# Decoding 64-bit weights with two VectorE instructions, and parts made on GpSimd and ScalarE

## The chip, the cores and the metric

The kernel runs on one core of a Trainium2 chip. The metric is the device time of one launch in microseconds (us). TensorE (PE in the profile) does the matrix products, VectorE (DVE), ScalarE (ACT) and GpSimd (POOL) work on elements, and SyncE (SP) issues most of the transfers (DMAs).

## The reference

The first half is a gated linear recurrence with a complex state, over 4 sequences, 8 heads, 768 steps and width 48; its output, laid out as 3072 tokens of 384, goes through a feed-forward layer.

```
mag = np.sqrt(a_re * a_re + a_im * a_im)
scale = np.minimum(mag, 0.999) / (mag + 1e-06)
a_re_n, a_im_n = (a_re * scale, a_im * scale)
for t in range(S):
    S_re, S_im = (ar * S_re - ai * S_im) + kv, ar * S_im + ai * S_re
    y[:, :, t] = np.einsum('bhd,bhde->bhe', q[:, :, t], S_re)
...
h = np.maximum(x @ w_in, 0.0)
return (h * h @ w_out).astype(np.float32)
```

The weights w_in (384 x 2048) and w_out (2048 x 384) arrive as 64-bit floats, which the kernel sees as pairs of 32-bit words, low and high. It must turn them into 32-bit floats on the chip.

## The kernel before

The tokens are worked in 12 groups, each of two chunks of 128 tokens. A group goes through these steps. Operands (23 small steps, `make_operands`): the gates are squared, limited and scaled on ScalarE and VectorE (`limit` and `lessened`, through the helper at L684, make two factors on ScalarE that `gates`, L750, reads, and `grown_factor`, L744, a third; `grown_squared`, L763, squares the key growth; `grow`, L770, is a scan of it); `totals`, `carries`, `carried` and `products` then form running products of the gates in a long row of short VectorE instructions (helper line L480, most of them with the names ab and pr), and end with the group's keys and queries, qk. Chunks: TensorE turns the keys (L878, tp), ScalarE copies them (L882 and L883, kt), TensorE makes scores (L871, a_ps), VectorE multiplies them by the mask (a<-a_ps,mask), TensorE makes the outputs (L863 and L897, y) and adds to the state (L918, add). GpSimd makes some small products of the last rows (L923 and L924, prod<-last), which wait for a transfer last<-qk. Then the feed-forward layer: the first product (L960, h_ps, eight pieces F0 to F7 of a group, which hold the buffers of h_ps two at a time), squared ReLU on ScalarE (L963 to L966, H), the second product. Groups 0 and 1 do the second product piece by piece with each w_out block (L976, o_ps, token T); later groups do it in seven smaller products over sums of halves (L1042). Outputs are copied from PSUM by ScalarE or added by VectorE (L996 to L998 and L1046 to L1066).

The weights come in 16 blocks of 128 x 768 pairs of words, eight of w_in (`order` "1") and then eight of w_out ("2"). `fetch` (L610) brings a block into one of three buffers called words; for w_in half of it goes through GpSimd's queue (token j, L632), the rest and all of w_out through SP's (token f, L626 and L632). `decode` (L579 to L595) turns a block into floats by five VectorE instructions: L586 and L588 build the head of the float from the high word (shift by 3, mask, sign), L590 keeps its power of two, L593 scales the low word with it, and the helper at L480 adds both into the weights w. `watch` (token W, L597 to L601) makes two ScalarE passes over each block, whose sums tell later whether the values lie in the range that this path handles; if they don't, a general path at the end of the program does everything anew. With these inputs it isn't entered.

The order of the work on all five engines is written out by hand. A string, FRONT (L1076), lists tokens, a letter and numbers each, and `follow` (L1196) issues them in turn: o0.8 is operand step 8 of group 0, a1.5 and b1.5 are chunk steps, l and i load a group's raw input (SP's and GpSimd's queue), D5 decodes block 5, W5 watches it, F0.6 is a piece of the first product, T0.0 one of the second. Each engine runs its instructions in the order in which they are issued. F0.k needs weights of D0 to Dk; T with index f needs D of 8 plus f. In the first stretch the tokens around the decodes run as follows; the full string has no decode beyond D15, which ends ahead of group 3.

```
D0 o0.9 o0.10 o0.6 o0.11 W0 W1 D1 o0.22 f3 v1 j3 o0.12 W2 o0.13 o0.15 o0.14 f4 j4 W3
l1 i1 o0.16 W4 o0.17 D2 o0.18 o1.6 o0.19 f5 j5 o0.20 o1.0 W5 a0.1 o1.3 o0.21 o1.1 D3
```

Of the kernel before, what the change touches and what calls it, by code (L numbers as in the profile page):

```python
# [23 lines left out]
I32 = mybir.dt.int32  # L24
U32 = mybir.dt.uint32
# [4 lines left out]
P = 128  # L30
# [395 lines left out]
def quotient_path(ctx, tc, feat, vtok, w_in, w_out, w1, w2, out, n_seq, count):  # L426
# [151 lines left out]
    order = "1111111122222222"  # L578
    def decode(dst, words, j):  # L579

        low, high = words[:, :, 0], words[:, :, 1]
        both = scr.tile([P, 2, E], I32, tag="work", name="decoded")
        head, rest = both[:, 0], both[:, 1]
        nc.vector.tensor_scalar(out=head, in0=high, scalar1=3, scalar2=0x3FFFFFF8,  # L586
                                op0=ALU.logical_shift_left, op1=ALU.bitwise_and)
        nc.vector.scalar_tensor_tensor(out=head, in0=high, scalar=-2 ** 30, in1=head,  # L588
                                       op0=ALU.bitwise_and, op1=ALU.bitwise_or)
        nc.vector.tensor_scalar(out=rest, in0=head, scalar1=-2 ** 23, scalar2=None,  # L590
                                op0=ALU.bitwise_and)
        rest = rest.bitcast(F32)
        nc.vector.scalar_tensor_tensor(out=rest, in0=low.bitcast(U32), scalar=2.0 ** -52, in1=rest,  # L593
                                       op0=ALU.mult, op1=ALU.mult)
        tt(dst, head.bitcast(F32), rest, ALU.add)  # L595
# [40 lines left out]
    def weights(i):  # L636
        if i in words_of:
            of_w2, j = block(i)
            decode(w2[:, 2 * j:2 * j + 2].rearrange("p k m -> p (k m)") if of_w2 else
                   w1[:, :, j * BLK:(j + 1) * BLK], words_of[i], i)  # L640
# [304 lines left out]

    h_ps, h_of, o_of, mix_of = {}, {}, {}, {}
# [16 lines left out]
    def squared_relu(i, f):  # L963
        h = h_of[i, f] = ffn.tile([P, 2, TOK], F32, name="h", bufs=NFB // 2 + 1)
        nc.scalar.activation(out=h, in_=h_ps[i, f], func=AF.Relu)  # L965
        nc.scalar.activation(out=h, in_=h, func=AF.Square)  # L966
# [29 lines left out]
    def end_of_second(i, b):  # L996
        out_of[i, b] = ffn.tile([P, DM], F32, name="o")
        nc.scalar.copy(out=out_of[i, b], in_=o_of[i, b])  # L998
# [47 lines left out]
    def outputs(i, r):  # L1046
# [6 lines left out]
        if r == 0:  # L1053
            nc.scalar.copy(out=o[0][:, left], in_=chain)
        elif r == 1:
            tt(o[0][:, left], others[0], o[0][:, left], ALU.add)
        elif r == 2:
            nc.scalar.copy(out=o[0][:, right], in_=chain)
        elif r == 3:
            nc.scalar.copy(out=o[1][:, right], in_=others[1])  # L1060
        elif r == 4:
            tt(o[1][:, right], chain, o[1][:, right], ALU.add)
        elif r == 5:
            tt(o[0][:, right], others[1], o[0][:, right], ALU.add)
        else:
            nc.scalar.copy(out=o[1][:, left], in_=chain)  # L1066
# [11 lines left out]
        "D0 o0.9 o0.10 o0.6 o0.11 W0 W1 D1 o0.22 f3 v1 j3 o0.12 W2 o0.13 o0.15 o0.14 f4 j4 W3 "  # L1078
        "l1 i1 o0.16 W4 o0.17 D2 o0.18 o1.6 o0.19 f5 j5 o0.20 o1.0 W5 a0.1 o1.3 o0.21 o1.1 D3 "
        "a0.2 a0.3 o1.4 o1.5 a0.4 a0.8 o1.2 o1.7 f6 j6 b0.0 a0.9 o1.8 b0.1 b0.2 b0.5 o1.9 b0.6 "  # L1080
        "D4 b0.3 b0.7 a0.0 b0.4 o1.10 W6 b0.8 o1.11 f7 j7 a0.5 o1.12 o1.22 a0.6 b0.9 o1.13 W7 "
        "a0.7 o1.15 o1.14 g0 v2 l2 i2 o1.16 F0.0 o1.17 F0.1 H0.0 D5 o1.18 F0.2 H0.1 o2.6 o1.19 "
        "f8 F0.3 H0.2 F0.4 H0.3 o1.20 o2.0 F0.5 H0.4 W8 a1.1 o2.3 o1.21 D6 a1.2 a1.3 o2.1 a1.4 "
        "a1.8 o2.4 o2.2 F0.6 D7 f9 H0.5 o2.5 a1.0 H0.6 a1.9 F0.7 a1.5 W9 f10 o2.7 a1.6 b1.1 "
        "a1.7 D8 b1.0 o2.10 o2.8 H0.7 b1.5 o2.9 f11 b1.6 D9 b1.2 b1.3 b1.7 T0.0 b1.4 g1 W10 "
        "o2.11 T0.1 W11 f12 F1.0 D10 o2.12 o2.22 F1.1 H1.0 D11 T0.2 H1.1 f13 W12 F1.2 o2.15 "
        "T0.3 H1.2 o2.13 F1.3 W13 f14 o2.16 o2.14 b1.8 F1.4 v3 H1.3 l3 b1.9 F1.5 H1.4 D12 W14 "
        "F1.6 D13 T0.4 f15 T1.0 H1.5 D14 F1.7 H1.6 T1.1 o3.6 o2.17 T1.2 H1.7 D15 W15 T1.3 o2.18 "
        "o2.19 T0.5 T0.6 t0 o3.0 T0.7 t1 T1.4 E0.0 t2 E0.1 s0.0 s0.1 o3.3 T1.5 o2.20 o3.4 o3.5 "
        "T1.6 o3.7 o3.1 o2.21 T1.7 o3.2 o3.10 a2.1 t3 E1.0 E1.1 s1.0 a2.2 s1.1 a2.0 o3.8 o3.9 "  # L1090
        "a2.3 a2.5 a2.4 a2.6 o3.11 a2.8 a2.7 b2.0 a2.9 o3.12 o3.22 b2.1 b2.5 b2.2 b2.6 o3.13 "
        "b2.3 b2.7 b2.4 g2 b2.8 o3.15 o3.14 v4 l4 F2.0 b2.9 F2.4 H2.0 o3.16 F2.1 H2.4 o3.17 "
        "F2.5 H2.1 X2.0 o3.18 Y2.0 o3.19 F2.2 H2.5 F2.6 H2.2 o4.6 o3.20 F2.3 H2.6 o4.0 F2.7 "
        "X2.1 o3.21 H2.3 Y2.1 o4.3 o4.1 X2.2 a3.1 Z2.0 o4.2 Y2.2 H2.7 a3.0 X2.3 o4.4 R2.0 Y2.3 "
        "a3.2 o4.5 a3.3 a3.5 Z2.1 a3.4 o4.7 a3.8 Q2.2 o4.10 Q2.1 R2.1 o4.8 a3.6 a3.9 Z2.2 a3.7 "
        "o4.9 Q2.3 Q2.0 b3.0 o4.11 R2.2 b3.1 Z2.3 b3.2 b3.5 o4.12 o4.22 o4.15 b3.6 R2.3 Z2.4 "
        "b3.7 g3 o4.13 Z2.5 R2.4 o4.14 o4.16 Z2.6 l5 b3.3 R2.6 R2.5 F3.0 b3.4 o4.17 b3.8 H3.0 "
        "F3.4 b3.9 o4.18 s2.0 o4.19 F3.1 H3.4 v5 s2.1 F3.5 H3.1 X3.0 o4.20 F3.2 H3.5 o5.6 F3.6 "
        "H3.2 X3.1 o4.21 o5.1 Y3.1 Y3.0 a4.1 F3.3 H3.6 X3.2 o5.2 Y3.2 F3.7 H3.3 a4.2 o5.0 a4.0 "
        "o5.3 H3.7 X3.3 o5.4 a4.3 Z3.0 a4.4 a4.5 o5.5 Y3.3 o5.7 a4.8 R3.0 a4.6 a4.9 o5.10 Z3.1 "  # L1100
        "a4.7 o5.8 o5.9 Z3.2 R3.1 Q3.2 Q3.1 Q3.0 Q3.3 o5.11 b4.0 R3.2 b4.1 b4.5 o5.12 Z3.3 "
        "o5.22 o5.15 b4.2 b4.6 R3.3 b4.3 b4.7 Z3.4 b4.4 g4 o5.13 b4.8 R3.4 o5.14 Z3.5 v6 b4.9 "
        "l6 o5.16 F4.0 Z3.6 H4.0 R3.5 o5.17 F4.4 R3.6 o5.18 s3.0 o5.19 s3.1 F4.1 H4.4 F4.5 H4.1 "
        "X4.0 o5.20 F4.2 H4.5 o6.6 F4.6 H4.2 X4.1 o5.21 Y4.1 o6.1 Y4.0 F4.3 H4.6 X4.2 o6.2 F4.7 "
        "Y4.2 H4.3 o6.0 a5.0 o6.3 H4.7 X4.3 o6.4 Z4.0 o6.5 a5.5 Y4.3 o6.7 a5.6 R4.0 Z4.1 a5.7 "
        "o6.10 o6.8 Z4.2 R4.1 Q4.2 o6.9 Q4.1 Q4.0 Q4.3 o6.11 b5.0 R4.2 Z4.3 b5.5 o6.12 o6.22 "
        "o6.15 b5.6 R4.3 Z4.4 b5.7 v7 g5 o6.13 Z4.5 R4.4 o6.14 o6.16 Z4.6 l7 F5.0 R4.5 R4.6 "
        "o6.17 F5.4 H5.0 o6.18 o6.19 F5.1 H5.4 s4.0 s4.1 F5.5 H5.1 X5.0 o6.20 F5.2 H5.5 o7.6 "
        "F5.6 X5.1 o6.21 H5.2 Y5.1 Y5.0 o7.1 a6.1 F5.3 H5.6 X5.2 o7.2 F5.7 Y5.2 H5.3 a6.2 a6.0 "
        "H5.7 X5.3 o7.0 a6.3 Z5.0 a6.5 a6.4 Y5.3 o7.3 a6.8 R5.0 o7.4 a6.6 a6.9 o7.5 Z5.1 a6.7 "  # L1110
        "o7.7 o7.10 Z5.2 R5.1 Q5.2 o7.8 Q5.1 Q5.0 Q5.3 o7.9 b6.0 o7.11 R5.2 b6.1 Z5.3 b6.2 b6.5 "
        "o7.12 b6.3 Z5.4 b6.4 o7.15 R5.3 o7.22 b6.6 b6.8 b6.7 g6 R5.4 Z5.5 o7.13 v8 Z5.6 b6.9 "
        "o7.14 R5.5 o7.16 s5.0 F6.0 R5.6 l8 o7.17 F6.4 H6.0 F6.1 H6.4 X6.0 o7.18 Y6.0 s5.1 F6.5 "
        "o7.19 H6.1 F6.2 H6.5 X6.1 F6.6 H6.2 Y6.1 o7.20 o8.6 F6.3 H6.6 o8.0 X6.2 o7.21 Y6.2 "
        "a7.1 o8.3 H6.3 F6.7 o8.1 Z6.0 H6.7 X6.3 o8.2 Y6.3 a7.0 R6.0 o8.4 a7.2 o8.5 a7.3 a7.5 "
        "Z6.1 a7.4 o8.7 Z6.2 R6.1 o8.10 Q6.2 Q6.1 o8.8 Q6.0 Q6.3 o8.9 a7.8 a7.6 a7.9 R6.2 Z6.3 "
        "a7.7 o8.11 b7.0 R6.3 o8.12 b7.1 b7.5 o8.22 Z6.4 o8.15 b7.2 b7.6 b7.3 b7.7 Z6.5 b7.4 g7 "
        "R6.4 o8.13 b7.8 R6.5 o8.14 Z6.6 v9 b7.9 s6.0 l9 o8.16 F7.0 R6.6 F7.4 H7.0 o8.17 F7.1 "
        "H7.4 X7.0 o8.18 s6.1 Y7.0 F7.5 o8.19 H7.1 F7.2 H7.5 X7.1 F7.6 H7.2 Y7.1 o8.20 o9.6 "
        "F7.3 H7.6 o9.0 X7.2 o8.21 Y7.2 a8.1 o9.3 H7.3 F7.7 o9.1 Z7.0 H7.7 X7.3 o9.2 Y7.3 a8.0 "  # L1120
        "R7.0 o9.4 a8.2 o9.5 a8.3 a8.5 Z7.1 a8.4 o9.7 Z7.2 R7.1 o9.10 Q7.2 Q7.1 o9.8 Q7.0 Q7.3 "
        "o9.9 a8.8 a8.6 a8.9 R7.2 Z7.3 a8.7 o9.11 b8.0 R7.3 o9.12 b8.1 b8.5 o9.22 Z7.4 o9.15 "
        "b8.2 b8.6 b8.3 b8.7 Z7.5 b8.4 g8 R7.4 o9.13 b8.8 R7.5 o9.14 Z7.6 v10 b8.9 s7.0 l10 "
        "o9.16 F8.0 R7.6 F8.4 H8.0 o9.17 F8.1 H8.4 X8.0 o9.18 s7.1 Y8.0 F8.5 o9.19 H8.1 F8.2 "
# [23 lines left out]
    def ranges(step):  # L1148
# [34 lines left out]
        "s": store,  # L1183
        "f": fetch,
        "j": lambda i: fetch(i, True),
        "i": lambda gi, part=None: load_parts(gi, part, True),
        "D": weights,
        "W": lambda i: watch(words_of[i], i) if i in words_of else None,
        "t": sum_weights,
# [70 lines left out]
```

## Time and profile before

| | us |
|---|---|
| median of 3 runs (701.58 to 702.04) | 701.61 |
| span of the profiled execution | 700.1 |
| what lies around the span, median less span | 1.5 |
| one decode on VectorE, start to the next start | 4.05 |
| VectorE busy in the first 200 us, by stages of 20 | 15.15, 19.03, 18.54, 18.75, 19.27, 18.06, 19.31, 19.10, 19.62, 14.43 |
| TensorE busy in the same stages | 0.47, 0, 6.82, 15.01, 16.10, 17.62, 20.00, 20.00, 20.00, 15.77 |
| TensorE busy from 200 to 650 | 448.90 |

The profile is of one execution, and its times count from the start of its span. A line such as `38.05 0.56 DVE L586 TENSOR_SCALAR decoded<-words 128x768 int32` is one instruction or a row of equal ones: start, duration, engine, line of the kernel, operation, output and inputs, shape and type, count; a bracket at its end gives the idle time of the engine ahead of it and what ended it. Records of the helper at L480 are told apart by their tiles.

### The profile page before, as it was taken

To read this page: it belongs to the slowest core of one execution; us is meant where nothing else is said; L and a number is where in the kernel's file an instruction comes from. 1 tells how busy PE (TensorE), PEld (TensorE's weight loads), DVE (VectorE), ACT (ScalarE), POOL (GpSimd) and SP (SyncE) were. 2 spreads that over 40 slices of the span, in tenths; PEclk is the share of its full clock that TensorE was granted. 3 is DMA by queue.
4 is the path that set the end of the run, shared out by engine and by line. 5 is a ranking of instruction groups with operands and counts; after the bars stand their busy time and mean duration, and the time that the engine had idled before them with its cause. 6 is when DMAs were issued, how large, how long until landed. Compare 5 with 4: busy or idle time off the path is not lost.

```text
span 700.1 us, 12510 instructions
## 1 busy us (share of the span) xinstructions
PE 624.7 (89%) x4955; PEld 548.4 (78%) x4955; DVE 529.8 (76%) x933; ACT 386.6 (55%) x684; POOL 33.0 (5%) x78
## 2 busy tenths in 40 slices
PE   0008779999889999999999999999999999999996
PEld 0007657775668998998989989989989989989896
DVE  7998998999698886895785885985985976972120
ACT  6757487653648538537557467376376476350230
POOL 6312200000000000000000000000000000000000
PEclk9999999999999999999999999999999999999999
DMA  8845543470253062071161151241230340110101
GB/s 209 200 89 111 120 109 104 144 147 10 60 96 47 2 111 55 4 139 24 30 113 24 31 111 25 60 87 20 70 82 15 82 76 9 30 23 2 29 1 28
DMA packets 44172, 47.75 MB, mean 68 GB/s; under 512 B 6024, under 2 KB 39112, under 8 KB 44104
## 3 DMA queue, kind: packets, MB, share of 16 engines
q1 hardware_dynamic: 41280, 41.20, 27.7%
q0 software_dynamic: 2336, 5.21, 3.3%
q8 instruction: 41, 0.67, 0.4%
q10 hardware_dynamic: 488, 0.44, 0.2%
q14 instruction: 27, 0.22, 0.1%
HBM read 36.18 MB, written 4.72 MB: 58 GB/s over the span
## 4 chain that ended last, share of the span: by engine, by line
PE 74%; DVE 12%; DMA 2%; SPq 1%; ACT 1%; issue 1%; POOL 0%; DVEq 0%
PE h_ps L960 30%; PE o_ps L1042 26%; PE a_ps L871 6%; PE y L897 3%; PE y L863 3%; PE add L918 2%; PE tp L878 2%; DVE qk L480 1%; DVE ab L480 1%; DVE room L480 1%; PE o_ps L976 1%; SPq L830 1%; DMA raw<-in_feat_dram 1%; DVE decoded L593 1%; DVE decoded L588 1%; DVE w L480 1%
## 5 line engine op out<-in xcount | busy, mean ns | idle before, releaser
L960 PE MATMUL h_ps<-x,w 128*128 128x256 f32 x1152 | 259.1, 385 | 7.2 <-DMA x<-x 5.4
L960 PEld LDWEIGHTS h_ps<-x,w 128*128 128x128 f32 x1152 | 221.1, 193 | 39.2 <-ACT qk L684 4.6
L965 ACT ACTIVATE h<-h_ps 128x512 f32<-128x512 f32 x96 | 57.5, 599 | 103.0 <-PE h_ps L960 94.6
L1042 PE MATMUL o_ps<-w,h 128*128 128x192 f32 x640 | 111.1, 328 | 0.0
L1042 PEld LDWEIGHTS o_ps<-w,h 128*128 128x128 f32 x640 | 103.6, 190 | 1.8 <-issue 0.9
L480 DVE TENSOR_TENSOR pr<-ab 128x384 f32<-128x384 f32 (+2 forms) x168 | 66.4, 413 | 4.4 <-ACT ab L758 0.5
L966 ACT ACTIVATE h<-h 128x512 f32<-128x512 f32 x96 | 60.6, 631 | 3.1
L480 DVE TENSOR_TENSOR a<-a_ps,mask 128x1024 f32<-128x1024 f32 x24 | 29.3, 1223 | 39.1 <-PE a_ps L871 39.1
L480 DVE TENSOR_TENSOR mix<-h 128x256 f32<-128x256 f32 x40 | 16.9, 422 | 55.2 <-ACT h L966 55.2
L878 PE MATMUL tp<-ident,qk 128*128 128x128 f32 x120 | 22.7, 301 | 39.6 <-DVE qk L480 37.7
L1042 PE MATMUL o_ps<-w_sum,mix 128*128 128x192 f32 x320 | 55.8, 328 | 0.0
L1042 PEld LDWEIGHTS o_ps<-w_sum,mix 128*128 128x128 f32 x320 | 52.0, 190 | 1.1 <-DVE state L480 0.7
L878 PEld LDWEIGHTS tp<-ident,qk 128*128 128x128 f32 x120 | 14.0, 148 | 45.8 <-issue 38.4
L480 DVE TENSOR_TENSOR ab<-pr 128x192 f32<-128x192 f32 (+1 forms) x180 | 45.8, 276 | 4.6
L480 DVE TENSOR_TENSOR qk<-ab,qk 128x768 f32<-128x768 f32 x48 | 44.9, 956 | 0.9
L684 ACT ACTIVATE qk<-raw 128x768 f32<-128x768 f32 x24 | 36.8, 1532 | 13.6 <-DVE raw L480 9.0
L976 PE MATMUL o_ps<-w,h 128*128 128x384 f32 x128 | 42.4, 488 | 0.0
L871 PE MATMUL a_ps<-qk 48*128 48x128 f32 x576 | 41.3, 293 | 0.0
L871 PEld LDWEIGHTS a_ps<-qk 48*128 48x128 f32 x576 | 36.5, 199 | 4.4 <-issue 4.3
L684 ACT ACTIVATE ab<-raw 128x768 f32<-128x768 f32 x24 | 37.1, 1564 | 2.3 <-DVE qk L480 2.3
L480 DVE TENSOR_TENSOR room<-ab,carry 128x1344 f32<-128x1344 f32 x24 | 36.2, 1552 | 2.2 <-ACT carry L799 2.2
L976 PEld LDWEIGHTS o_ps<-w,h 128*128 128x128 f32 x128 | 24.1, 190 | 16.2 <-DVE w L480 0.7
(106 smaller groups left out, 810.7 us busy)
## 6 DMA issues: line engine op xcount, KB each, us to landing
raw<-in_feat_dram SPq DMA_DIRECT2D x40, 288.0 KB
words<-in_moe_w_out_dram SPq DMA_DIRECT2D x8, 768.0 KB
last<-qk SPq DMA_DIRECT2D x72, 64.5 KB
vt<-in_vtok_dram SPq DMA_DIRECT2D x24, 192.0 KB
out_dram<-o SPq DMA_DIRECT2D x23, 192.0 KB
raw<-in_feat_dram SPq DMA_DIRECT2D x120, 32.0 KB
words<-in_moe_w_in_dram POOLq DMA_DIRECT2D x8, 192.0 KB, 5.1
words<-in_moe_w_in_dram SPq DMA_DIRECT2D x8, 192.0 KB
```

Of the source, the lines that this page charges most:

```text
L480: nc.vector.tensor_tensor(out=out, in0=in0, in1=in1, op=op)
L684: nc.scalar.activation(out=out.rearrange("p c j n -> p c n j"), func=AF.Copy, in_=in_.rearrange("p c (n j) -> p c n j", j=L), **kwargs)
L863: nc.tensor.matmul(ys[p_ % 2][crossed(hh, p_), p_ // 2], lhsT=states[b][1 - c_seq % 2][rows(hh), c, p_], rhs=operand(c, p_, rows(hh)), sta ...
L871: nc.tensor.matmul(ps[:, hh, p_], lhsT=operand(2 + c, p_, rows(hh)), rhs=operand(c, p_, rows(hh)), start=(c == RE), stop=(c == IM))
L878: nc.tensor.transpose(tp[:, g], operands[gi][:, 2 + c, b, g, 0:C], ident)
L897: nc.tensor.matmul(tiles["y"][p_ % 2][crossed(hh, p_), p_ // 2], lhsT=v[:, at:at + ROWS], rhs=tiles["am"][:, hh, p_], start=(first and p_ ...
L918: nc.tensor.matmul(add[rr, c, p_], lhsT=kt[c][:, p_, rr], rhs=v[:, at:at + D], start=True, stop=True)
L960: nc.tensor.matmul(ps[:, j], lhsT=w1[:, g, (2 * f + j) * P:(2 * f + j + 1) * P], rhs=x_of[i][:, g], start=(g == 0), stop=(g == NG - 1))
L965: nc.scalar.activation(out=h, in_=h_ps[i, f], func=AF.Relu)
L966: nc.scalar.activation(out=h, in_=h, func=AF.Square)
L976: nc.tensor.matmul(o_of[i, b], lhsT=tokens_of(i, f, b)[:, j], rhs=w2[:, k], start=(k == 0), stop=(k == NFB - 1))
L1042: nc.tensor.matmul(to, lhsT=x(k)[:, j], rhs=factor(z)[:, 2 * k + j], start=(z in (0, 1, 3) and k == j == 0), stop=(k == KH // 2 - 1 and j ...
```

## The change

The low halves and the signs of a block's words are now prepared by two other engines, in a new step `parts` (token U), 16 of them. It writes one 32-bit word for each weight: GpSimd fills its lower 16 bits with the rounded low word times 2^-29, and ScalarE its upper 16 bits with the sign of the high word as a 16-bit float, plus or minus one. There are two such buffers, used in turn. `decode` shifts the high words left by three into the weights' own memory and adds the prepared words to them as 32-bit integers, which is built as one instruction over half-words. The result is the weight with an exponent smaller by one: half the weight.

The factor 2 comes back later: by the scale of the ReLU, and by a factor in the copies and additions of the outputs.

In FRONT, U0 comes directly ahead of D0, U1 directly after D0, and each further U(i+1) directly after D(i), from U2 after D1 to U15 after D14; nothing else in the string is moved. On ScalarE, U0 and U1 so stand between `limit` and `lessened` of group 0, U2 ahead of its `grown_squared`, U4 ahead of the copy of the first turned keys of group 0, U5 after group 1's `lessened`, U7 after W8 and ahead of the copy of the first keys of group 1. On GpSimd, U0 to U2 stand behind j2 and ahead of j3, U3 behind group 1's loads, U4 behind j5, U5 behind j6, U6 and U7 behind group 2's loads, and U8 to U15 after the small products of group 1.

```diff
+    def parts(i):
+        if i not in words_of:
+            return
+        low, high = words_of[i][:, :, 0], words_of[i][:, :, 1]
+        if not parts_of:
+            parts_of["room"] = scr.tile([P, 2, E], I32, tag="work", name="part")
+        two = parts_of[i] = parts_of["room"][:, i % 2]
+        nc.gpsimd.tensor_scalar(out=two.bitcast(I16).rearrange("p (e h) -> p e h", h=2)[:, :, 0],
+                                in0=low.bitcast(U32), scalar1=2.0 ** -29, scalar2=0.0,
+                                op0=ALU.mult, op1=ALU.add)
+        nc.scalar.activation(out=two.bitcast(BF16).rearrange("p (e h) -> p e h", h=2)[:, :, 1],
+                             in_=high.bitcast(F32), func=AF.Sign)
     def decode(dst, words, j):
-        low, high = words[:, :, 0], words[:, :, 1]
-        both = scr.tile([P, 2, E], I32, tag="work", name="decoded")
-        head, rest = both[:, 0], both[:, 1]
-        nc.vector.tensor_scalar(out=head, in0=high, scalar1=3, scalar2=0x3FFFFFF8,
-                                op0=ALU.logical_shift_left, op1=ALU.bitwise_and)
-        nc.vector.scalar_tensor_tensor(out=head, in0=high, scalar=-2 ** 30, in1=head,
-                                       op0=ALU.bitwise_and, op1=ALU.bitwise_or)
-        nc.vector.tensor_scalar(out=rest, in0=head, scalar1=-2 ** 23, scalar2=None,
-                                op0=ALU.bitwise_and)
-        rest = rest.bitcast(F32)
-        nc.vector.scalar_tensor_tensor(out=rest, in0=low.bitcast(U32), scalar=2.0 ** -52, in1=rest,
-                                       op0=ALU.mult, op1=ALU.mult)
-        tt(dst, head.bitcast(F32), rest, ALU.add)
+        nc.vector.tensor_scalar(out=dst, in0=words[:, :, 1], scalar1=3, scalar2=None,
+                                op0=ALU.logical_shift_left)
+        tt(dst, dst, parts_of[j], ALU.add)
...
+    of_w1, of_w2 = [1.0 if w.dtype == F32 else 2.0 for w in (w_in, w_out)]
+    def twice(out, x):
+        nc.scalar.activation(out=out, in_=x, func=AF.Copy, scale=of_w2)
+    def add_twice(x, y):
+        nc.vector.scalar_tensor_tensor(out=y, in0=x, scalar=of_w2, in1=y, op0=ALU.mult, op1=ALU.add)
...
-        nc.scalar.activation(out=h, in_=h_ps[i, f], func=AF.Relu)
+        nc.scalar.activation(out=h, in_=h_ps[i, f], func=AF.Relu, scale=of_w1)
...
-        nc.scalar.copy(out=out_of[i, b], in_=o_of[i, b])
+        twice(out_of[i, b], o_of[i, b])
...
-            tt(o[0][:, left], others[0], o[0][:, left], ALU.add)
+            add_twice(others[0], o[0][:, left])
...
-        "D0 o0.9 o0.10 o0.6 o0.11 W0 W1 D1 o0.22 f3 v1 j3 o0.12 W2 o0.13 o0.15 o0.14 f4 j4 W3 "
+        "U0 D0 U1 o0.9 o0.10 o0.6 o0.11 W0 W1 D1 U2 o0.22 f3 v1 j3 o0.12 W2 o0.13 o0.15 o0.14 "
...
+        "U": parts,
```

The four other lines of `outputs` with a copy or an addition change in the same way.

## The prediction

> **What bounds the kernel now.** I read the busy totals first, then the busy time of each engine by stage, then the order of time of the engines in the stages that are not full, and last the chain of waits.
>
> ```profile
> PE 624.7 (89%) x4955; PEld 548.4 (78%) x4955; DVE 529.8 (76%) x933; ACT 386.6 (55%) x684; POOL 33.0 (5%) x78
> ```
>
> VectorE looks second, 76%. The stages tell more; the columns are the stretch, then busy time of PE, PE's weight loads, DVE, ACT and POOL in its 20 us, then granted clock, DMA share and GB/s.
>
> ```profile
> 20.00:40.00 20.00, 0.00 (x0) 0.00 (x0) 19.03 (x41) 13.11 (x29) 7.54 (x14) 1.00 0.86 190
> 40.00:60.00 20.00, 6.82 (x68) 5.96 (x70) 18.54 (x21) 12.19 (x16) 4.10 (x8) 1.00 0.43 89
> ...
> 100.00:120.00 20.00, 17.62 (x224) 14.62 (x225) 18.06 (x24) 14.44 (x26) 0.78 (x2) 0.91 0.47 134
> 120.00:140.00 20.00, 20.00 (x78) 14.54 (x77) 19.31 (x26) 14.19 (x29) 0.00 (x0) 1.00 0.41 133
> 140.00:160.00 20.00, 20.00 (x108) 14.97 (x108) 19.10 (x37) 9.71 (x14) 0.00 (x0) 1.00 0.64 129
> 160.00:180.00 20.00, 20.00 (x64) 11.79 (x63) 19.62 (x22) 8.78 (x18) 0.00 (x0) 1.00 0.08 20
> ```
>
> To about 100 us VectorE is the full engine and TensorE starves; from 119.25 to 183 TensorE has no gap, so VectorE, though 97% busy, sets nothing. From 200 to 650 TensorE is busy 448.90 of 450. Sixteen decodes are spread over 13.7 to 164 us; only those of the first stage can be worth time. One block, on VectorE's timeline (start, duration, line, shapes):
>
> ```profile
> 38.05 0.56 DVE L586 TENSOR_SCALAR decoded<-words 128x768 int32<-128x768 int32 x1
> 38.64 0.96 DVE L588 SCALAR_TENSOR_TENSOR decoded<-words,decoded 128x768 int32<-128x768 int32 x1
> 39.64 0.56 DVE L590 TENSOR_SCALAR decoded<-decoded 128x768 int32<-128x768 int32 x1
> 40.23 0.96 DVE L593 SCALAR_TENSOR_TENSOR decoded<-words,decoded 128x768 f32<-128x768 uint32 x1
> 41.22 0.96 DVE L480 TENSOR_TENSOR w<-decoded 128x768 f32<-128x768 f32 x1
> ```
>
> 38.05 to the next start at 42.10: 4.05 us a block, 65 us for 16. The chain of waits (a start, a length, what) passes the seventh block and then stays on TensorE:
>
> ```profile
> 98.61 0.97 DVE decoded L588
> ...
> 101.19 0.97 DVE w L480
> 102.15 0.04 issue
> 102.20 4.25 PE h_ps L960 x12
> ```
>
> **What the Trainium skill says.** "SBUF — State Buffer", section "Who interferes with whom": VectorE and GpSimd share one port pair, an exclusive lock held for a whole instruction; a VectorE instruction with two SBUF inputs contends with a GpSimd instruction that reads SBUF, and whichever starts first blocks the other fully. The trace of before agrees, for GpSimd as the loser:
>
> ```profile
> 56.78 0.61 POOL L923 COPY prod<-last 128x4 f32<-128x4 f32 x1 [13.69 <-DMA last<-qk]
> 57.37 0.22 POOL L924 TENSOR_SCALAR prod<-last 128x2 f32<-128x2 f32 x1
> ```
>
> That copy usually takes 0.19 us; it ended at 57.39, with VectorE's L730 (56.38, 0.96). That VectorE can be the loser the trace doesn't show: GpSimd's reads are tiny. The same section has ScalarE on ports of its own. "GPSIMD Engine Reference", section 3.1, gives the only price for a GpSimd pass over 768 elements: 1.03 to 2.6 cycles an element at 1.2 GHz, estimated 0.66 to 1.66 us; "VectorE: DVE Perf Modes", section "Mode 2×_2P", says a one-source op runs doubled where the outermost dimensions suit, as L586 (0.56) against L588 (0.96) does.
>
> **The change part by part.**
>
> Removed: per block five VectorE instructions, 4.05.
>
> Added on VectorE: one shift and one integer add. For a w_out block the shift is contiguous: 0.56. For a w_in block it writes 3×256 out of rows of 2048, so I take the undoubled 0.96. The add, over 768 words with two inputs, has no row: not below the 0.96 of other two-input passes, and at most 1.76 (L480 over 1536 elements), since it is built over 1536 half-words. I take 0.99 with spacing. So 1.98 for w_in (2.07 saved), 1.57 for w_out (2.48 saved): 8×2.07 + 8×2.48 = 36 us of VectorE.
>
> Added on ScalarE: 16 Sign passes over words. L744, 128x768, ends 0.75 before its successor starts (65.35, 66.10): 16×0.75 = 12 us. No new table load; I find none in the instruction order.
>
> Added on GpSimd: 16 passes, reading 768 words. Price P: from 0.66 to 1.66 by the skill, plus 0.19 for a tiny op's fixed part, so 0.66 to 1.85; I take 1.3, about the middle. While it holds the lock VectorE's two-input work stands, and that work fills VectorE almost wholly, so I charge P to VectorE. Bounds: 0 if GpSimd always loses and fits gaps, 1.85 if always first.
>
> Factor 2: Relu with scale, copies as activations (0.48 for 128x384 either way), additions as scalar_tensor_tensor (the same rate as L480 by the rows above): nothing, and after 201 us they lie beside full TensorE. SP's and TensorE's orders are unchanged. On GpSimd's queue the passes stand ahead of fetches j3 to j7 and of the carried products; the latest is U4 ahead of the latter. GpSimd idles 13.69 before 56.78, so each goes unnoticed.
>
> Walk of the start, shift against before, without contention (P on top later):
> - Group 0: the second block's Sign (U1) stands on ScalarE ahead of `lessened` (before: the second of two L684 rows that end at 17.19) and waits for words last issued at 11.87+0.51; with the page's 5.1 to landing that is 17.5 at most, about 16.9. `lessened` ends about 19.2, the gates start 19.3 instead of 17.79; U2 stands ahead of `grown_squared`. The scan of `grow` comes at about 27.2 instead of 25.37: +1.8. Both blocks' savings before it are lost to these waits.
> - D2 on the full VectorE: −2.07. Shift −0.3.
> - U4's Sign is ahead of the first keys' copy (51.98), where ScalarE is the late one: +0.75, on to scores and the masked product (60.66, which waited 1.43 for TensorE, so D3's saving is worth nothing): +0.45.
> - D4 −2.07, but the next masked product (69.38) waits for scores, which are at 67.41+1.06 plus the shift: about −0.4.
> - D5 −2.07: keys of group 1 at about 95 instead of 97.29. ScalarE then has W8 and U7's Sign (+0.75) before it copies them (97.89): first product after it 102.20 → 101.1 to 102.0. Shift −0.2 to −1.1; the first second-product instruction (119.25) follows with it.
> - 119 to 183: TensorE full, the w_out blocks save 20 us of VectorE for nothing, but group 2's carried rows come earlier, so this wait goes:
>
> ```profile
> 185.45 0.29 PE L863 MATMUL y<-last,state 48*64 48x128 f32 x1 [0.98 <-DMA last<-qk]
> ```
>
> −0.98. Other gaps to 201 hang on masks and rows just made on VectorE and stay.
>
> Sum without contention: −1.2 to −2.1, say −1.6.
>
> With P: U3 falls in group 0's totals and U4 in its carried products: +2P on the keys. U5 falls in D4 and the gates: +P. U6, U7 in group 1's totals and carried: +2P. The masked product is then VectorE's own again, so D4 counts in full. Sum: −0.3 +0.75 −2.07 −2.07 +0.2 (ScalarE late with W8) + 5P −0.98 = 5P − 4.5. At 1.3: +2.0 us. Profiled: 700.1 span plus the 1.5 around it is the median 701.61; 700.1+2.0 = 702.1, with 1.5 again **703.6**.
>
> **The rivals.**
> - *GpSimd loses, or P is under 0.6*: the one lock, decided the other way, at U3 to U7. For it: every collision seen in before was lost by GpSimd. Against it: VectorE leaves about 0.03 us between its instructions, and whoever is queued starts there. Time 701.6−1.6 = 700.0, **faster**; the crossing from 703.6 is at 5P = 4.5, P = 0.9.
> - *Between, P 0.63 to 1.18*: 5P−4.5 from −1.4 to +1.4: no change, 701.6.
> - *VectorE's relief pays in full*: −36, 665. TensorE has only some 68 us of idle time in its first 200 us (the stages' busy times of PE sum to 132), nearly all before 119, and its order is unchanged; fetches, keys and scores stand in that chain. Nearly excluded.
> - *The add runs as 1536 elements*: +0.8 at D2, D4 and D5, 2.4 on top: 706.0.
>
> **How the numbers follow.** About 0.2%, 1.4 us, is what a measurement can tell from no change. Contention with P over 1.18 (the slow add in it): 0.50. Between: 0.27. GpSimd loses: 0.21. Relief in full: 0.02. So faster 0.23, same 0.27, slower 0.50. Likeliest 703.6, its own range 703.0 to 706.4 (P=1.85: 5×1.85−4.5=+4.8). The range runs from 699.5 (the −2.1 end) to 706.4; the slow add's far end, the relief and the far end of the no-contention case are left out.
>
> **What would show it.** Right: VectorE instructions of 0.96 that last over 2 us beside GpSimd passes at U3 to U7; U1's Sign ending just before `lessened`; TensorE's first o_ps later than 119.25; the decode at two instructions. Wrong: passes that stretch over several VectorE instructions while those keep 0.96 (GpSimd loses); passes below 0.9; an add well over 0.96; TensorE gaps after 119 that before doesn't have.

## The result, and the profile after

| | before | changed |
|---|---|---|
| median, us | 701.60 (4 runs, 701.34 to 702.04) | 707.65 (4 runs, 707.21 to 709.03) |
| ratio, 95% interval | | 1.0083 [1.0068, 1.0098] |
| span of the profiled execution | 700.1 | 707.2 (its own time 709.03) |

The change is 6.05 us slower, where 2.0 was forecast. The sign was right; the time lies above the range's end of 706.4. The medians and ratios in this document are of undisturbed executions.

The totals of the profile after (page, first part), then its stages; the columns are those of the lines shown of before.

```profile
PE 625.7 (88%) x4955; PEld 549.6 (78%) x4955; DVE 500.0 (71%) x885; ACT 400.1 (57%) x700; POOL 53.2 (8%) x94
```

```profile
20.00:40.00 20.00, 0.00 (x0) 0.00 (x0) 17.27 (x28) 16.56 (x31) 9.70 (x16) 1.00 0.83 182
40.00:60.00 20.00, 3.58 (x38) 2.79 (x38) 17.13 (x24) 13.09 (x23) 3.84 (x7) 1.00 0.40 87
...
100.00:120.00 20.00, 16.82 (x200) 13.90 (x200) 11.49 (x14) 17.25 (x30) 2.95 (x5) 1.00 0.41 103
120.00:140.00 20.00, 17.12 (x96) 12.20 (x93) 16.55 (x20) 17.23 (x31) 5.02 (x4) 0.91 0.50 170
```

VectorE lost 30 us of work and TensorE still starves longer: VectorE is no longer full in the stages shown (11.49 of 20 from 100 to 120), so it waits, and from 100 to 140 ScalarE has become the busiest of the three, 17.25 and 17.23. The groups of the changed instructions, with least, middle and greatest duration in ns:

```profile
L591 POOL TENSOR_SCALAR part<-words x16: 1039/1174/2299, 14.1 to 165.3; 128x768 int16<-128x768 uint32 x16
L594 ACT ACTIVATE part<-words x16: 1043/1060/1107, 15.9 to 165.2; 128x768 bf16<-128x768 f32 x16
L481 DVE CUSTOM_DVE_ANT_0 w<-w,part x16: 957/959/959, 17.0 to 166.7; 128x1536 uint16<-128x1536 uint16 x16
```

The add takes 0.96, the lower of its two bounds; Sign takes 1.06 (its successor starts about 0.93 after it) where 0.75 was taken; the GpSimd pass takes 1.04 to 1.17 where it isn't held up.

What TensorE waited for between 60 and 130 us (the table of waits: total, times, longest), and the two rows of the first product in order of time:

```profile
PE h_ps L976 <- DVE w L481: 4.6, 1, 4.6
PE h_ps L976 <- DMA x<-x: 3.7, 1, 3.7
PE tp L886 <- ACT kt L891: 3.4, 2, 1.8
```

```profile
78.85 7.27 PE L976 MATMUL h_ps<-x,w 128*128 128x256 f32 x26 [3.67 <-DMA x<-x]
90.69 12.50 PE L976 MATMUL h_ps<-x,w 128*128 128x256 f32 x46 [4.56 <-DVE w L481]
```

Each piece of the first product is 12 matmuls here. After 26 of them, two into the third piece, TensorE stops until VectorE's add of the sixth block has ended (89.67 and 0.96). The third piece needs the third block, which was decoded 46 us earlier. In before the first four pieces, 48 matmuls from 76.82 on, have no gap, and the next wait is short and for another engine:

```profile
90.83 5.45 PE L960 MATMUL h_ps<-x,w 128*128 128x256 f32 x24 [1.27 <-ACT h L965]
```

On VectorE of the changed kernel the reverse stands, the seventh and eighth add waiting for TensorE:

```profile
103.31 0.96 DVE L481 CUSTOM_DVE_ANT_0 w<-w,part 128x1536 uint16<-128x1536 uint16 x1 [0.79 <-PE h_ps L976]
104.30 0.95 DVE L601 TENSOR_SCALAR w<-words 128x768 int32<-128x768 int32 x1
111.40 0.96 DVE L481 CUSTOM_DVE_ANT_0 w<-w,part 128x1536 uint16<-128x1536 uint16 x1 [6.14 <-PE h_ps L976]
```

The shift of the same block (104.30) waits for nobody; only the add does. None of these three waits is in the trace of before. The chain of waits, which passed the old decode before, now names Sign (ACT part) three times ahead of what TensorE waits for:

```profile
90.69 7.33 PE h_ps L976 x22
...
103.85 0.96 ACT part L594
104.80 0.32 ACT kt L890
...
118.47 0.98 ACT part L594
119.45 0.68 ACT room L752
120.13 1.46 ACT room L692
...
124.16 0.86 ACT part L594
125.02 0.32 ACT kt L890
125.33 0.20 ACT kt L891
125.58 0.55 PE tp L886 x3
```

Milestones, each the start of an instruction in the profiled executions of before and after, and the shift between them: scan of group 0 25.37, 28.19 (+2.8); first key turn 50.71, 53.08 (+2.4); second 52.74, 55.98 (+3.2); scan of group 1 72.03, 75.17 (+3.1); first key turn of group 1 97.29, 103.02 (+5.7); first second-product instruction 119.63, 125.97 (+6.3); first product of group 2 200.88, 208.12 (+7.2). The profiled execution of the changed kernel is its longest, 1.4 us over the median, and runs 0.28 us behind that of before even ahead of the first Sign (ScalarE's L692 at 14.54, in before L684 at 14.26).

VectorE itself ends the keys of group 1 only 2.6 us later than before, at 99.80 instead of 97.24 (the first row is of before); TensorE, still busy with the pieces that it was held up in, turns them at 103.02:

```profile
93.42 3.82 DVE L480 TENSOR_TENSOR qk<-ab,qk 128x768 f32<-128x768 f32 x4
95.99 3.81 DVE L481 TENSOR_TENSOR qk<-ab,qk 128x768 f32<-128x768 f32 x4
```

### The profile page after: what moved, and what is told of

It reads as the page before. It is cut to its first block, busy times and chain, and to the rows that moved or that the text cites. A ratio compares the mean times of both kernels' runs of the same rounds, so it can differ in the third digit from the quotient of the medians.

```text
span 707.2 us, 12528 instructions
## 1 busy us (share of the span) xinstructions
PE 625.7 (88%) x4955; PEld 549.6 (78%) x4955; DVE 500.0 (71%) x885; ACT 400.1 (57%) x700; POOL 53.2 (8%) x94
## 4 chain that ended last, share of the span: by engine, by line
PE 79%; DMA 7%; ACT 5%; DVE 5%; SPq 2%; issue 1%; DVEq 0%; ACTq 0%
PE h_ps L976 33%; PE o_ps L1058 26%; PE a_ps L879 7%; DMA raw<-in_feat_dram 5%; PE y L905 3%; PE add L926 3%; PE y L871 3%; PE tp L886 2%; PE o_ps L992 2%; DMA words<-in_moe_w_in_dram 1%; DVE qk L481 1%; DVE room L481 1%; ACT qk L692 1%; DVE w_sum L481 1%; DMA words<-in_moe_w_out_dram 1%; ACT part L594 1%
## 5 line engine op out<-in xcount | busy, mean ns | idle before, releaser
L1058 PEld LDWEIGHTS o_ps<-w,h 128*128 128x128 f32 x640 | 103.6, 190 | 1.8 <-issue 0.9
L481 DVE TENSOR_TENSOR mix<-h 128x256 f32<-128x256 f32 x40 | 16.9, 422 | 55.2 <-ACT h L982 55.2
L957 ACT ACTIVATE o<-o_ps 128x192 f32<-128x192 f32 (+1 forms) x44 | 15.3, 350 | 71.6 <-PE o_ps L1058 68.6
L481 DVE TENSOR_TENSOR ab<-pr 128x192 f32<-128x192 f32 (+1 forms) x180 | 47.3, 285 | 4.6
L481 DVE TENSOR_TENSOR room<-ab,carry 128x1344 f32<-128x1344 f32 x24 | 37.8, 1617 | 6.7 <-ACT carry L807 6.6
L692 ACT ACTIVATE qk<-raw 128x768 f32<-128x768 f32 x24 | 36.7, 1528 | 8.9 <-DVE raw L481 7.4
L692 ACT ACTIVATE ab<-raw 128x768 f32<-128x768 f32 x24 | 37.0, 1559 | 2.3 <-DVE qk L481 2.3
```

Source lines behind the costliest of these rows:

```text
L481: nc.vector.tensor_tensor(out=out, in0=in0, in1=in1, op=op)
L692: nc.scalar.activation(out=out.rearrange("p c j n -> p c n j"), func=AF.Copy, in_=in_.rearrange("p c (n j) -> p c n j", j=L), **kwargs)
L1058: nc.tensor.matmul(to, lhsT=x(k)[:, j], rhs=factor(z)[:, 2 * k + j], start=(z in (0, 1, 3) and k == j == 0), stop=(k == KH // 2 - 1 and j ...
```

## The theory and the experiments

**Theory A**: three causes stand beside the shorter decode. (1) The add over a w_in block, whose three stretches lie 2048 words apart, is ordered against everything between the first and the last of its bytes, so against TensorE's reads of other blocks; the expectations call this a false ordering. (2) Sign passes stand ahead of factors and key copies in ScalarE's order, one of them with a wait for arriving words. (3) GpSimd's passes hold the port pair. **Rivals**: the port is the whole loss; or VectorE's relief is hidden anyway, so nothing can be gained by mending (1) to (3). A third, TensorE's granted clock, had no experiment; the part on the prediction says what the runs tell of it.

**e1: weights block by block.** The tile w1 is laid out so that a block is contiguous.

```diff
-    lhsT=w1[:, g, (2 * f + j) * P:(2 * f + j + 1) * P]
+    lhsT=w1[:, f, (2 * g + j) * P:(2 * g + j + 1) * P]
...
-    w1[:, :, j * BLK:(j + 1) * BLK].bitcast(I32)
+    w1[:, j].bitcast(I32)
```

> The changed kernel with the w_in weights kept block by block in memory, so that each block's shift and add write one contiguous stretch. Nothing else differs. Theory A (false ordering): in the changed kernel the add over a strided stretch is ordered against everything between its first and its last byte, so the third piece of the first product waits for the add of the sixth block (4.6 us of TensorE idle up to 90.69) and the seventh and eighth adds wait for TensorE (0.8 and 6.1 us). Then this kernel has none of the three waits, its first second-product instruction comes at about 122.5 instead of 125.97, and it takes 704.0 us (703.3 to 704.8). The shifts fall from 0.95 to 0.56 besides. Rival B (port contention and ScalarE's passes are the whole loss): the waits merely show other delays, only the shorter shifts help, some 0.4 us at each of three places on the path: 706.5.

Measured: 704.73 (703.71 to 708.49, 7 runs), ratio 1.0053 [1.0034, 1.0073]. TensorE's rows at the same place:

```profile
89.12 8.07 PE L976 MATMUL h_ps<-x,w 128*128 128x256 f32 x36 [1.60 <-ACT h L981]
98.56 0.55 PE L886 MATMUL tp<-ident,qk 128*128 128x128 f32 x3 [1.37 <-DVE qk L481]
```

The wait for VectorE's add is gone; TensorE is ready for group 1's keys before they are, and turns them at 98.56 instead of 103.02. VectorE's waits of 0.79 and 6.14 are gone too. Against the changed kernel that is 2.9 us by the medians, and 704.73 lies in the expected range. The first second-product instruction came at 124.12 and not at 122.5.

**e11: three adds.** The layout stays; the one add becomes three, each over one stretch.

```diff
-        tt(dst, dst, parts_of[j], ALU.add)
+            for g in range(NG):
+                tt(dst[:, g], dst[:, g], parts_of[j][:, g * BLK:(g + 1) * BLK], ALU.add)
```

> The changed kernel with the add of each w_in block made as three adds, one for each of the three stretches that it writes in the old layout; nothing else differs, the shift is as slow as in the changed kernel and VectorE has more to do (three short adds, about 0.4 us each, for one of 0.96). Theory A (the one add over a strided stretch is ordered against all that lies between its ends): TensorE's 4.6 us wait for the sixth block's add and VectorE's 6.1 us wait for TensorE go, as in the first experiment, 705.3 (704.3 to 706.3). Rival (the first experiment gained by its shorter shifts or by the other memory layout): 707.7 to 709.

Measured: 705.88 (704.29 to 707.43, 4 runs), ratio 1.0058 [1.0037, 1.0080]. The rows of the first product:

```profile
78.61 10.89 PE L980 MATMUL h_ps<-x,w 128*128 128x256 f32 x36 [3.88 <-DMA x<-x]
89.77 8.07 PE L980 MATMUL h_ps<-x,w 128*128 128x256 f32 x36 [0.26 <-ACT h L985]
```

Same shift, same layout, same ScalarE and GpSimd, and the 4.6 us wait is 0.26 for another engine. The group 1 keys are turned at 99.73 (+2.4 against before, where the changed kernel had +5.7). So (1) is shown: the waits come from the one add over the strided block, not from the shift's length or from the layout alone. What it is worth is less sure: 1.8 us by the medians of four runs each, whose ranges just touch (e11 to 707.43, the changed kernel from 707.21), 2.9 in e1 with the shorter shifts. Whether the compiler or the chip sets this order the runs don't show.

**e5: the first Signs moved.** On e1's layout; G is the Sign, L the GpSimd pass of U.

```diff
-U0 D0 U1 o0.9 o0.10 o0.6 o0.11 W0 W1 D1 U2 o0.22 f3 v1 j3 o0.12 W2
+L0 L1 o0.9 o0.10 G0 D0 G1 o0.6 o0.11 W0 W1 D1 L2 o0.22 f3 v1 j3 o0.12 G2 W2
```

> The kernel with weights block by block, and of the three first Sign passes the first two moved behind the two factors of group 0's gates and the third behind its growth factors; GpSimd's passes stay. Theory A's second part (the head): the gates no longer wait for the second block's words, so they start at 17.8 as in the kernel before; the scan of group 0 still stands behind two more ScalarE passes, at about 26.5 instead of 27.9; 703.3 (702.5 to 704.2), and its runs spread by less than 2 us instead of the 4.8 of the first experiment, since no arrival of a transfer stands ahead of the gates. Rival (the head is hidden by later waits): 704.7 with the same spread.

Measured: 702.79 (700.98 to 703.46, 12 runs), ratio 1.0006 [0.9996, 1.0016]. The scan of group 0 starts at 26.09 (27.89 in e1) and the whole is 1.9 us shorter by the medians; the spread is 2.5 us instead of 4.8 (under 2 was expected). One more expectation was off: the gates still start late, since the first add stands ahead of them on VectorE and now waits for the moved Sign. How long the second Sign waits for its words differs from run to run. In the changed kernel and in e2, ScalarE's rows:

```profile
17.69 1.07 ACT L594 ACTIVATE part<-words 128x768 bf16<-128x768 f32 x1 [0.76 <-DMA words<-in_moe_w_in_dram]
```

```profile
20.19 1.07 ACT L595 ACTIVATE part<-words 128x768 bf16<-128x768 f32 x1 [3.88 <-DMA words<-in_moe_w_in_dram]
```

**e2: GpSimd's pass for two blocks only.**

```diff
-        nc.gpsimd.tensor_scalar(...)
+        if i < 2:
+            nc.gpsimd.tensor_scalar(...)
```

> The changed kernel with GpSimd's pass made for the first two blocks only; the later ones reuse what these left in the two buffers, so the lower halves of 14 blocks are left out. ScalarE's passes, the adds and their order stay. Theory A with port contention as a second part: the four VectorE instructions that were lengthened by 0.7 to 0.8 us ahead of the sixth block (beside the third, fourth, fifth and seventh pass) go back to their length, so the sixth add comes about 3 us earlier, and TensorE's wait on it with it: 704.6 (703.8 to 705.4). Rival B2 (contention is the whole loss of 6): 701.6. Rival C (VectorE's lost time is hidden behind ScalarE and TensorE): 707.

Measured: 707.35 (702.42 to 709.11, 11 runs), ratio 1.0071 [1.0052, 1.0090]. By its number it is rival C's 707, and the expected 704.6 failed. The trace reads otherwise: in the profiled execution the words came 2.5 us later (the row above), so the scan of group 0 started at 30.70 instead of 28.19, and yet TensorE went on behind the sixth add at 90.74, as in the changed kernel (90.69). The passes' 2.5 us were gained between, and the late words took them. Why the words came late isn't shown, and the runs spread over 6.7 us, so the time alone decides nothing. The same edit is tried again in e12, where no arrival stands ahead of the gates.

**e3 and e4: GpSimd's passes alone, and the Signs alone, in the kernel before.** Each adds its half of `parts` at the places of the change; nobody reads what is written.

```diff
+    def parts(i):
+        ...
+        nc.gpsimd.tensor_scalar(out=two..., in0=low..., ...)      # e3
+        nc.scalar.activation(out=two..., in_=high..., func=AF.Sign)      # e4
```

> The kernel before with GpSimd's 16 passes added at the places that the change gives them, into a buffer that nobody reads. Theory (contention, 0.75 a pass as seen in the changed kernel): five passes meet a busy VectorE ahead of 100 us, at most 5 x 0.75 = 3.8, of which waits for TensorE at the scores hide one or two: 703.5 to 705. If contention follows the recorded prediction (1.3 a pass): 706 to 708. If GpSimd always loses: 701.6.

Measured: 713.03 (712.00 to 714.65, 4 runs), ratio 1.0167 [1.0148, 1.0185]: more than any of the numbers. Up to group 1's keys the shift is +4.8: seven VectorE rows (the first at 14.88, 18.09 and 21.56) are longer by 0.66 to 0.80 each, where the expectation had counted five passes. The rest comes later, where VectorE, 97% busy in before, has no room for eight more passes and TensorE begins to wait for the old decode, 2.4 us in all; what lies beyond that wasn't followed. TensorE's rows:

```profile
127.87 2.85 PE L991 MATMUL o_ps<-w,h 128*128 128x384 f32 x8 [0.52 <-DVE w L481]
136.31 2.85 PE L991 MATMUL o_ps<-w,h 128*128 128x384 f32 x8 [0.41 <-DVE w L481]
157.42 5.43 PE L991 MATMUL o_ps<-w,h 128*128 128x384 f32 x16 [1.46 <-DVE w L481]
```

In the changed kernel TensorE has no wait of this kind from 104 to 212, so this part is not in its 6 us.

> The kernel before with ScalarE's 16 Sign passes added at the places that the change gives them, into a buffer that nobody reads. Theory (the head is ScalarE's): the second pass waits for the second block's words ahead of a factor of the gates, the third stands ahead of the growth factors, so the scan of group 0 comes at about 28 instead of 25.4, +2.6, and the fifth pass adds 0.9 at the copy of the first keys; here all of the old decodes still stand behind: 704.5 to 705.5. Rival (ScalarE has slack, 55 per cent busy): under 702.3.

Measured: 708.47 (707.06 to 708.65, 4 runs), ratio 1.0090 [1.0074, 1.0107]. The scan of group 0 came at 28.98 (+3.6), and again TensorE waits 1.67 and 1.58 us for key copies that stand behind a Sign (0.77 and nothing in before). The Signs cost 6.7 us on their own, 3 more than the expected range allows; the places after 100 us were not in the expectation.

**e7 and e10: the new decode for w_out only, then two Signs moved.** In e7 the first eight blocks keep the old decode; e10 puts the Sign of block 9 behind W9 and that of block 10 behind W10.

```diff
-            decode(w2[:, 2 * j:2 * j + 2]... if of_w2 else w1[...], words_of[i], i)
+            (decode if of_w2 else decode_before)(w2[:, 2 * j:2 * j + 2]... if of_w2 else w1[...], words_of[i], i)
```

```diff
-a1.5 W9 f10 ... D8 U9 b1.0 ... D9 U10 b1.2 ... g1 W10
+a1.5 W9 G9 f10 ... D8 L9 b1.0 ... D9 L10 b1.2 ... g1 W10 G10
```

> The changed kernel with the old five-instruction decode for the eight w_in blocks and the new one for the eight w_out blocks only (and the factor 2 only on the outputs). No part of the start is touched. Recorded prediction's step: TensorE is full from 119 to 183, 20 us less of VectorE buy only the 0.98 us that TensorE waits for the last rows at 185.45: 700.7 (700.2 to 701.4). Rival: the passes of blocks 8 to 11 come ahead of a key copy or a factor between 100 and 125 and cost 1 to 2 us: 702.5 to 703.5.

> The seventh run's kernel (new decode for w_out blocks only) with two Sign passes moved: that of block 9 behind its watch, that of block 10 behind its watch. Theory (the 2 us between the first product's seventh piece and the first second product were Sign passes ahead of group 1's second chunk's key copies and factors): first second-product instruction at 119.3 to 120 instead of 121.58, 700.9 (700.2 to 701.6). Rival (TensorE's slower clock after its waits, or GpSimd's passes of those blocks): 702.5 as before.

Measured: e7 702.86 (700.80 to 708.77, 12 runs), ratio 1.0013 [0.9992, 1.0034]; e10 701.28 (699.84 to 703.78, 12 runs), ratio 0.9986 [0.9973, 0.9999]. e7's first product up to its seventh piece is on time (102.12 against 102.20), the first second-product instruction is +1.95. Of TensorE's rows there, e7 first, then e10:

```profile
121.19 0.55 PE L904 MATMUL tp<-ident,qk 128*128 128x128 f32 x3 [1.56 <-ACT kt L909]
121.58 5.33 PE L1010 MATMUL o_ps<-w,h 128*128 128x384 f32 x16
```

```profile
120.10 0.55 PE L906 MATMUL tp<-ident,qk 128*128 128x128 f32 x3
120.49 5.37 PE L1012 MATMUL o_ps<-w,h 128*128 128x384 f32 x16
```

The wait for the key copy is gone with the two Signs. The rival of e7 was right: these late Signs cost 1.6 us by the medians of 12 runs each, and eat up what the w_out blocks bring.

**e6, e8, e9: passes moved to where engines idle.** e6 moves the passes of ten blocks (0 to 4 and 7 to 11) and some watches and decodes, on e1's layout; e8 takes two faults out of e6; e9 is e8's order with the old decode, old layout and no passes.

```diff
 e6
-o0.8 U0 D0 U1 o0.9 o0.10 o0.6 o0.11 W0 W1 D1 U2 o0.22 f3 v1 j3 o0.12 W2 o0.13 ...
+G0 L0 o0.8 o0.9 D0 o0.10 L1 G1 o0.11 D1 o0.22 o0.12 o0.6 W0 f3 v1 j3 L2 o0.13 ...
-D3 U4 ... H0.3 o1.20 o2.0 F0.5 H0.4 W8 a1.1 ... D6 U7 ... D7 U8 f9 H0.5 o2.5 a1.0 H0.6 a1.9 F0.7
+o1.6 W4 G4 ... D3 ... H0.3 G7 o1.20 o2.0 F0.5 H0.4 a1.1 ... D6 ... f9 L7 L8 H0.5 o2.5 G8 a1.0 H0.6 W8 a1.9 D7 D8 F0.7
 e8
-o0.10 L1 G1 o0.11 D1 o0.22 o0.12 o0.6 W0 f3 v1 j3 L2 o0.13 ... o1.6 W4 G4 o0.19 ... o1.0 W5 a0.1
+o0.10 o0.11 L1 o0.22 o0.12 G1 o0.6 W0 f3 v1 j3 L2 o0.13 D1 ... o1.6 o0.19 ... o1.0 a0.1 ... o1.2 G4 ... o1.8 W4 ... o1.14 W5
```

> The kernel with weights block by block, and the Sign passes, GpSimd's passes, a few watches (first, second, fourth, fifth, ninth) and the decodes 0, 1, 7 and 8 put where ScalarE and VectorE idle in the traces so far, none of them ahead of a factor or a copy of keys that VectorE or TensorE waits for. If the new ScalarE passes' places and GpSimd's port are all that stands against the shorter decodes, the scan of group 0 comes at 23.5 (25.4 before), group 1's keys some 3 us ahead of the kernel before, TensorE's first second-product instruction at 117 (119.6 before): 699.0 (698.0 to 700.5). If VectorE's relief can't be turned into time at all because fetches and scores hold the start: 701 to 702.

Measured: 701.78 (698.59 to 706.37, 20 runs), ratio 1.0003 [0.9989, 1.0018]. Missed. The scan of group 0 came at 23.41 as expected, but the keys' second turn at 53.16, later than before: In ScalarE's order the fifth block's watch, which waited for its words until 44.92 (0.35 us), its Sign, the real parts and the sixth block's watch all stand ahead of the first key copy, which ran at 52.41; TensorE had turned these keys at 48.32 and waited 3.96 us for that copy.

```profile
44.92 0.90 ACT L609 ACTIVATE size<-words 128x768 bf16<-128x768 f32 x1 [0.35 <-DMA words<-in_moe_w_in_dram]
...
46.88 1.05 ACT L596 ACTIVATE part<-words 128x768 bf16<-128x768 f32 x1
47.80 1.45 ACT L709 ACTIVATE room<-raw 128x1536 f32<-128x1536 f32 x1
49.17 0.88 ACT L609 ACTIVATE size<-words 128x768 bf16<-128x768 f32 x1
```

> The moved kernel of the sixth run, with two things taken away that its trace shows: the second block's Sign and decode now come behind the growth factors and the scan of group 0, so no arrival of words stands ahead of it; and the fifth block's watch and Sign (which waited for words until 44.92 and then pushed the real parts and the first key copy to 53.16) come behind the key copies, the sixth's watch later still. Theory (arrivals of words on ScalarE's in-order queue cause both the spread and the lost 3 us at the keys): second key turn at about 50 instead of 53.16, runs spread by less than 3 us instead of 8, 698.5 (697.3 to 699.8). Rival (the spread is TensorE's clock episodes and not the words): the spread stays at 5 or more, 700 to 702.

Measured: 696.99 (695.84 to 700.31, 4 runs), ratio 0.9921 [0.9892, 0.9950]: faster than both kernels. In the profiled execution, the longest of the four, the second turn came at 52.11, not at 50, so that number of the expectation failed; group 1's keys are turned at 95.12, the first second-product instruction is at 117.03 (119.63 before). The spread is 4.5 us over four runs, not under 3: arrivals aren't all of it.

> Control for the eighth run: the kernel before with the old five-instruction decode and no Sign or GpSimd passes, but with the watches and decodes at the eighth run's places. If the eighth's time is due to the shorter decode and not to the moves, this one is at or above 701.6 (701 to 704, since 7 and 8 are decoded later); if the moves themselves do it, it is below 700.5.

Measured: 707.67 (705.51 to 708.18, 5 runs), ratio 1.0065 [1.0040, 1.0090]. The moves alone lose 5.8 (701.88 is the median of before measured beside it); the new decode at these places, with e1's layout, is worth 10.7 us (707.67 less 696.99), and at the least 5.2 (705.51, the shortest of e9, less 700.31, the longest of e8).

**e12: e8 with GpSimd's pass for two blocks only.**

> The kernel of the eighth run with GpSimd's pass for the first two blocks only (the lower halves of the other 14 are left from these two). No arrival of words stands ahead of the gates here, unlike in the second run, so this tells what GpSimd's passes cost. Contention at 0.7 to 0.8 a pass for about four passes ahead of group 1's keys, of which the waits for scores and key copies hide half: 695.6 (694.8 to 696.6) beside 697.0. If contention is wholly hidden: 697. If each pass costs the 1.3 of the recorded prediction at five places: 691.

Measured: 695.01 (694.01 to 696.23, 4 runs), ratio 0.9908 [0.9890, 0.9926]. That is 2.0 us less than e8 by the medians (1.4 was expected), but the ranges of the four runs each overlap. The traces say it more plainly. Ahead of the first key turn three VectorE rows of e8 are each 0.67 longer than in e12, one at 29.75 and these two (e8 first, then e12):

```profile
43.15 2.22 DVE L481 TENSOR_TENSOR ab<-room 128x1344 f32<-128x1344 f32 x1
45.41 4.48 DVE L481 TENSOR_TENSOR qk<-ab,qk 128x768 f32<-128x768 f32 x4
```

```profile
42.13 1.56 DVE L481 TENSOR_TENSOR ab<-room 128x1344 f32<-128x1344 f32 x1
43.73 3.81 DVE L481 TENSOR_TENSOR qk<-ab,qk 128x768 f32<-128x768 f32 x4
```

The scan of group 0 is 0.33 later in e8 than in e12 and the first key turn 2.35 (50.04, 47.69): these 2.0 us are the three passes. So contention isn't hidden, and it is far from 1.3 at five places, 6.5.

## Why the prediction was right or wrong

**What bounds the kernel; relief in full.** Right. VectorE lost 30 us of busy time and nothing of it came back as time in the changed kernel; with w_out alone (e7, e10) at most 0.6 us did (701.88, before measured beside e10, less 701.28), and in e8, with the passes moved, 4.9 (701.88 less 696.99).

**The failed step: "The add, over 768 words with two inputs, has no row: not below the 0.96 of other two-input passes, and at most 1.76".** The add was priced by its length alone, and the walk let TensorE's pieces of the first product follow their own blocks ("SP's and TensorE's orders are unchanged"), so that D5's shorter decode set when TensorE turned group 1's keys. The length was right, 0.96. What it missed is that the one add over a strided block is ordered against reads of other blocks: TensorE stood 4.56 us, VectorE 0.79 and 6.14, and TensorE turned the keys 3.2 us after VectorE had ended them (103.02, 99.80). In e1 and e11 the waits are gone and the time falls by 2.9 and 1.8 us. That it is the stretch from first to last byte, and not the whole tile, is read from the row of 26 matmuls: the first group of the third piece lies outside the sixth block's first-to-last stretch and ran, the next lies inside and waited.

**"Shift −0.2 to −1.1; the first second-product instruction (119.25) follows with it."** Failed too. (119.25 is the key turn ahead of it; the instruction itself starts at 119.63.) Between the seventh piece and that instruction two Signs stand ahead of a factor and a key copy (the chain at 118.47 and 124.16), which the prediction didn't walk: e7 against e10, 1.6 us, and the same wait of 1.56 in the changed kernel, in e1 and in e4 (1.58). In the changed kernel's trace this shows little (+5.7 at the keys, +6.3 at that instruction), since before's seventh piece ran at a low clock, 4.25 us for 12 matmuls, and the changed kernel's in 2.86.

**The head, +1.8.** Right mechanism, undersized: +2.8 at the scan. The words were there at 17.69, not 16.9, and each of the two Signs takes 0.93 in line and not 0.75. U2's pass lengthened a row of the gates by 0.68 (2.44 for 1.76), but not the way to the scan, where VectorE waits 1.80 for ScalarE. e5 gave 1.9 us of it back. That this wait makes the time depend on an arrival wasn't foreseen.

**GpSimd and the port, P = 1.3 at five places.** Mechanism right, and VectorE is the loser, as the Trainium skill has it ("SBUF — State Buffer", "Who interferes with whom": whichever starts first blocks the other). VectorE's rows of the changed kernel beside the pass at 38.15 and behind that at 84.05, each with its like that met no pass:

```profile
38.14 1.16 DVE L481 TENSOR_TENSOR ab<-pr 128x48 f32<-128x48 f32 x2
...
39.80 0.33 DVE L481 TENSOR_TENSOR ab<-pr 128x48 f32<-128x48 f32 x2
```

```profile
83.34 0.36 DVE L481 TENSOR_TENSOR ab<-pr 128x192 f32<-128x192 f32 x1
...
84.33 1.05 DVE L481 TENSOR_TENSOR ab<-pr 128x192 f32<-128x192 f32 x1
```

0.33 became 1.16 and 0.36 became 1.05. A pass lengthened VectorE by 0.68 to 0.83, less than the 1.04 to 1.19 that it took itself, so the price was about 0.75 and not 1.3. U5 met no busy VectorE but its wait for scores. U3, U4, U6 and U7 cost 0.83, 0.79, 0.69 and 0.80, 3.1 for the 6.5 of 5P, and the 3.4 too much hid part of what was missed.

**D3 and D4 worth nothing or full.** D3's saving was indeed lost to the scores (VectorE waits 2.04 for a_ps at 63.92). D4's was also: "The masked product is then VectorE's own again, so D4 counts in full" failed, it waited 1.24 for scores, and the state behind it 0.65 for TensorE.

**"−0.98".** It became 0.45 (192.68 waits that long for the last rows). But the same wait is 0.25 in e7's execution and 1.59 in e10's, which have the same decodes, so no gain can be told from one execution.

Added up to the end of group 1's keys on VectorE, the prediction's terms are −0.3 + 0.75 − 2.07 − 2.07 + 6.5 = +2.8, and the measured shift is +2.6. That is luck: the head cost 1.0 more and D4's 2.07 were lost, against 3.4 too much for the port. That the kernel without the false ordering takes 704.73 (e1), near the forecast of 703.6, is luck of the same kind, with the late Signs at nothing besides. The causes are not a clean sum: 2.9 (ordering, e1), 1.9 (head, e5), 1.6 (late Signs, on another kernel) and 2.0 (port, on another kernel) are 8.4, against which stand some of the shorter decodes.

**What stays open.** The clock granted to TensorE falls for some us in every profiled execution but that of e12 (read from 44 to 140 us). In before it was 0.71 and 0.87 from 100 to 108 us; in the changed kernel 0.79 and 0.78 from 76 to 84, 0.57 and 0.58 from 88 to 96, 0.76 and 0.81 from 124 to 132. The second of these follows the wait of 4.56: the 46 matmuls after it took 0.27 us each, where e1 and e11, at a clock of 1.00 there, took 0.22. That is about 2.2 us, an estimate, of the 3.2 by which TensorE turned the keys late. So the gain of e1 and e11 is that of the waits and of this slow stretch together, less a slow stretch of their own from 100 to 108 (0.70 and 0.50; 0.69 and 0.50). Whether a wait brings a slow stretch on isn't shown: the wait of 4.20 at 76.82 in before is followed by none.

The clock alone doesn't make the 6 us. Of 78 executions of before on record, 23 had a mean clock of 0.987 or less, as three of the four of the changed kernel had, and these took 701.66 to 704.69; the shortest of the changed kernel is 707.21. Of the spreads, that of e8 goes with the mean clock (695.84 and 696.44 at 0.994, 697.55 at 0.992, 700.31 at 0.987), that of e6 doesn't (699.19 at 0.985, 706.37 at 0.997), and its cause stays open.

## What to carry to other kernels

A cheaper instruction is to be checked for what it is ordered against, not only for its length: look in the trace of the changed kernel for waits between instructions that share a tile but no bytes, and make written stretches contiguous. Work that is moved to an engine with idle time (ScalarE was 55% busy) is free only behind what others wait for; ahead of a factor or a key copy a pass of 1.06 us costs up to its length (two cost 1.6 us in e7), and a wait for an arriving transfer on an in-order engine holds back all behind it. With e1's layout and its passes in the idle places the same change gained 0.8% (e8; e9 for what the moves alone do).

## What the runs showed of the hardware that wasn't expected

- The integer add of 768 words on VectorE, built over 1536 half-words, takes 0.96 us, the same as a 32-bit float pass over 768 elements with two inputs. In three parts it takes 1.09 together, only 0.13 more:

```profile
89.39 1.09 DVE L481 CUSTOM_DVE_ANT_0 w<-w,part 128x512 uint16<-128x512 uint16 x3
```

- The shift takes 0.55 us with a contiguous output and 0.95 into three stretches of a wider row.
- GpSimd's pass over 768 words, 32-bit to 16-bit with stride, takes 1.04 us alone and up to 2.30 beside VectorE's two-input rows (the pass at 90.71).
- A ScalarE pass that writes every other 16-bit half takes 1.06 us for 768 elements; passes that write 32-bit words take 0.85, and the watch's pass, which reads the same words and writes 16-bit numbers without gaps, 0.88 (L607).
